# Four small tables padded in SBUF, so that every large tile begins on a multiple of 512 bytes

## The chip, the core and the metric

The kernel runs on one core of a Trainium2 chip. The metric is the time of one execution on the device, in microseconds. TensorE (PE; its weight loads are PEld) multiplies, VectorE (DVE), ScalarE (ACT) and GpSimd (POOL) do the element-wise work, and SyncE (SP), ACT and POOL issue DMA transfers, which 16 DMA engines carry out. SBUF is the on-chip memory, 128 partitions wide; an address below is a byte offset within each partition.

## The reference

Two layers follow each other. The first is a retention layer over 4 sequences of 768 steps, with 8 heads of width 64, and a state that decays by a factor gamma of its own for each head:

```python
for t in range(S):
    state = gamma[None, :, None, None] * state + np.einsum('bhd,bhe->bhde', k[:, :, t], v[:, :, t])
    y[:, :, t] = scale * np.einsum('bhd,bhde->bhe', q[:, :, t], state)
```

Its output, as 3072 rows of 512, goes through a feed-forward layer with a hidden width of 2048, whose negative hidden values are scaled by a factor `alpha` for each hidden column:

```python
h = x @ w_in
g = np.maximum(h, 0.0) + alpha * np.minimum(h, 0.0)
return g @ w_out
```

## The kernel before, in words

**Tiling.** The 3072 rows are twelve units of 256 steps, three to a sequence, and six blocks of two units. A unit is not walked step by step. Keys and queries are scaled by powers of gamma out of a table `tab` (`rescale`, line 145, tile `kdq`, f16), turned so that the head width lies on the partitions (tile `kq`), and multiplied with each other (`score_mm`, line 250). A mask in the table `mi` keeps the causal half (`masks`, line 263). The output of the unit is the masked scores times the values plus the queries times the state so far (`out_mm`, lines 281 and 296); the state is updated once for each half unit from key-value products (`sum_mm`, line 208; `state`, lines 228 to 238, tiles `ss`, `tf`, `tg`). `mi` also holds the identity for TensorE's transposes.

**Feed-forward.** Each block goes through `ffn1` (line 324; in halves, `ffn1_unit`, line 364, for block 1) with `w_in` as the stationary operand, an activation on ACT and one DVE instruction that uses `oma_sb` (one minus alpha), and then `ffn2` (line 395) with `w_out`, an ACT copy (line 404, tile `os`) and a store of 256 KB (line 408).

**Turning.** Units 0 to 3 are turned on TensorE (`turn_pe`, line 175, with an ACT copy, line 181). Units 4 to 11 are turned by a DMA transpose of the whole `kdq` tile into `kq` (`turn_dma`, line 165), which SP issues.

**Order.** The order is written out by hand (`manual_schedule`): the instructions of each engine run in the order of the code, and generators (`gen`, `half`, advanced by `tick`) put the feed-forward matmuls of one block between the retention work of the next. SP's queue holds, in this order, the loads of k, q and v for the units (line 125), the DMA transposes and the stores. POOL's queue holds rescales, state copies and the issue of the weight loads, which turn f32 into f16 on the way (lines 421 and 425). ACT's queue begins with the loads of `tab`, `mi` and `alpha` (lines 429 to 431). Around the second place that the prediction speaks of, the order on SP is: transpose of unit 4, loads of unit 6, the last three stores of block 0, transpose of unit 5, loads of unit 7.

**Placement.** All SBUF tiles come from one pool, which lays them one behind the other in the order of their creation, each rounded up to 32 bytes; the first lies at 16512. In the program before, the tiles begin here:

| tile | bytes per partition | begins at | past a multiple of 512 |
|---|---|---|---|
| tab | 208 | 16512 | 128 |
| mi | 768 | 16736 | 352 |
| alpha | 512 | 17504 | 96 |
| spin | 1024 | 18016 | 96 |
| warm | 4 | 19040 | 96 |
| oma | 64 | 19072 | 128 |
| win | 16384 | 19136 | 192 |

`wout`, the tiles `tg`, and all the buffers for loads, `kdq`, `kq`, `vx`, `xT`, `gt`, `hm`, `os` and the others follow `win`. Each of them is a multiple of 512 bytes, so each begins 192 bytes past a multiple of 512.

**What a DMA moves.** A load of k, q or v moves runs of 512 bytes (two steps of one head, f32) into a partition's row of 4096. A store moves rows of 2048 bytes out of `os`. A DMA transpose moves pieces of 256 bytes. A weight load reads runs of 1024 or 2048 bytes and writes half of that.

Of the kernel before, what the change touches and what calls it, by code (L numbers as in the profile page):

```python
# [9 lines left out]
FP = mybir.dt.float32  # L10
F16 = mybir.dt.float16
# [7 lines left out]
def kernel(  # L19
# [13 lines left out]
    NFT = d_ff // 128  # L33
# [10 lines left out]
    p_ar = np.arange(128, dtype=np.float64)  # L44


    OQ, OD, OI = 2 * H, 4 * H, 4 * H + NP
    NTAB = OI + NFT
    tab_np = np.zeros((128, NTAB), dtype=np.float64)
    for h in range(H):  # L50
        for r in range(2):
# [6 lines left out]
    tab_np[0:NFT, OI : OI + NFT] = np.eye(NFT)  # L58
    tab_np = tab_np.astype(np.float32)

    mi_np = np.zeros((128, 384), dtype=np.float16)
    pm = (p_ar % 64)[:, None]
    for rj in range(2):
        for ri in range(2):
# [7 lines left out]
    sbp = ctx.enter_context(tc.tile_pool(name="sbp", bufs=1, space=bass.MemoryType.SB))  # L72
    psp = ctx.enter_context(tc.tile_pool(name="psp", bufs=1, space=bass.MemoryType.PSUM))
    ctx.enter_context(tc.manual_schedule())

    tab = sbp.tile([128, NTAB], FP, tag="tab", name="tab")
    mi = sbp.tile([128, 384], F16, tag="mi", name="mi")
    mask = mi[:, 0:256].rearrange("p (r i) -> p r i", r=2)
    ident = mi[:, 256:384]
    dec = tab[:, OD : OD + NP].unsqueeze(2).to_broadcast([128, NP, 64])  # L80
    alpha_sb = sbp.tile([NFT, 128], FP, tag="alpha", name="alpha")
    spin = sbp.tile([128, 512], F16, tag="spin", name="spin")
    warm = sbp.tile([128, 1], FP, tag="warm", name="warm")
    oma_sb = sbp.tile([128, NFT], FP, tag="oma", name="oma")
    w_in_all = sbp.tile([128, 4, d_ff], F16, tag="win", name="win")
    w_out_all = sbp.tile([128, NFT, d_model], F16, tag="wout", name="wout")

# [539 lines left out]
```

## Time and profile before

| | |
|---|---|
| time, median of 3 runs | 226.14 us (225.40, 226.14, 226.42) |
| the profiled execution | 225.29 us, of which the span from first to last instruction is 223.5 us |
| granted TensorE clock, mean | 0.981 |
| PE busy | 205.9 us (92%) |
| DVE, ACT, POOL busy | 117.5, 101.2, 81.5 us |
| DMA | 34.01 MB in 62791 packets, of which 18081 under 512 bytes |
| queue q1 (SP): loads, stores, transposes | 57696 packets, 29.37 MB, 52.1% of 16 engines' span |
| queue q0 (POOL): weights | 4752 packets, 4.19 MB, 12.5% |
| queue q10 (ACT): tab, mi, alpha | 320 packets, 0.13 MB, 0.3% |

The span is drawn in 40 slices of 5.6 us; a digit is a busy share in tenths. PEclk is the share of its full clock that TensorE was granted. A packet is one contiguous piece of a transfer on one DMA engine; the DMA share of a stretch can exceed 1, since packets on one engine overlap. The chain is the work that ended last, followed back from the end of the program: at each step to what released it. An idle time in brackets is that of the engine just before the instruction, with what ended it.

### The profile page before, as it was taken

The page shows a single profiled execution, that of the slowest core. Times are in us where ns is not written, and L with a number is a line of the kernel's source. Part 1 is how long each engine was busy: PE and PEld are TensorE (multiplying, and loading weights), DVE is VectorE, ACT ScalarE, POOL GpSimd, SP SyncE. Part 2 cuts the span into 40 slices and gives each one's busy share as a digit, 9 for nine tenths or more (in the row PEclk, how much of TensorE's full clock was granted, in tenths as well). Part 3 has the DMA queues.
Part 4 walks back from the last instruction along what each step waited for, and adds up shares of the span by engine and source line. Part 5 has one row for each costly group of instructions (what it writes and reads, how often), then busy time and mean ns, then how long its engine had stood idle before and what let it go on. Part 6 is the DMA issues. An engine that isn't in the chain of part 4 may idle for free.

```text
span 223.5 us, 5019 instructions
## 1 busy us (share of the span) xinstructions
PE 205.9 (92%) x2100; PEld 109.7 (49%) x2100; DVE 117.5 (53%) x194; ACT 101.2 (45%) x168; POOL 81.5 (36%) x104
## 2 busy tenths in 40 slices
PE   7766798979899995999999999999999999999992
PEld 2445543547657743444455544545544555444440
DVE  3573198555753862118884058764088832388000
ACT  2544576425737513157613366414466242676121
POOL 2499302262039787800039920069700340000000
PEclk9998899999999999799999999999999999999998
DMA  6999999945696999939992169981190021100111
GB/s 183 298 182 123 204 226 276 245 83 94 163 290 165 198 325 215 269 92 237 242 261 96 49 142 269 219 221 47 62 218 5 4 91 53 47 3 0 47 73 68
DMA packets 62791, 34.01 MB, mean 152 GB/s; under 512 B 18081, under 2 KB 59697, under 8 KB 62769
## 3 DMA queue, kind: packets, MB, share of 16 engines
q1 hardware_dynamic: 57696, 29.37, 52.1%
q0 software_dynamic: 4752, 4.19, 12.5%
q8 instruction: 16, 0.26, 0.5%
q10 hardware_dynamic: 320, 0.13, 0.3%
q14 instruction: 7, 0.05, 0.1%
HBM read 27.40 MB, written 6.29 MB: 151 GB/s over the span
## 4 chain that ended last, share of the span: by engine, by line
PE 80%; DMA 6%; ACT 5%; POOL 4%; SPq 2%; issue 1%; DVE 1%; DVEq 0%; ACTq 0%; POOLq 0%
PE ops L395 34%; PE hps L324 31%; PE hps L364 6%; DMA kq<-kdq 3%; PE y L296 3%; DMA qs<-in_q_dram 2%; PE y L281 2%; SPq L125 2%; PE st L208 2%; ACT xT L309 2%; ACT kq L181 1%; PE sca L250 1%; ACT vx L159 1%; POOL kdq L145 1%; POOL tg L238 1%
## 5 line engine op out<-in xcount | busy, mean ns | idle before, releaser
L395 PE MATMUL ops<-wout,gt 128*128 128x512 f16 x384 | 89.5, 385 | 0.6 <-DVE gt L335 0.6
L335 DVE SCALAR_TENSOR_TENSOR gt<-hm,oma,hps 128x512 f16<-128x512 f32 x80 | 59.3, 747 | 43.4 <-ACT hm L334 35.5
L324 PE MATMUL hps<-xT,win 128*128 128x512 f16 (+1 forms) x336 | 71.1, 373 | 1.4 <-ACT xT L309 1.4
L395 PEld LDWEIGHTS <-gt 128*128 128x128 f16 x384 | 36.4, 99 | 43.2 <-issue 3.2
L334 ACT ACTIVATE hm<-hps 128x512 f32<-128x512 f32 x80 | 47.5, 597 | 20.7 <-PE hps L324 20.6
L324 PEld LDWEIGHTS <-win 128*128 128x128 f16 x336 | 33.3, 99 | 37.9 <-issue 1.4
L404 ACT ACTIVATE os<-ops 128x512 f32<-128x512 f32 x24 | 14.2, 599 | 59.7 <-PE ops L395 59.7
L145 POOL TENSOR_TENSOR kdq<-qs,tab 128x512 f16<-128x512 f32 (+1 forms) x16 | 24.4, 1528 | 19.8 <-DMA qs<-in_q_dram 19.7
L238 POOL CAST tg<-tf 64x256 f16<-64x256 f32 x40 | 16.2, 405 | 35.7 <-DVE tf L228 33.8
L263 DVE TENSOR_TENSOR m<-sca,mi 128x512 f16<-128x512 f32 x24 | 16.5, 686 | 23.1 <-PE scb L250 23.1
L232 POOL TENSOR_TENSOR tf<-ss,tab 128x256 f32<-128x256 f32 x16 | 9.8, 610 | 42.3 <-DVE ss L231 41.5
L309 ACT ACTIVATE xT<-y 128x512 f16<-128x512 f32 x24 | 16.0, 738 | 18.7 <-PE y L296 18.7
L376 DVE SCALAR_TENSOR_TENSOR gt<-hm,oma,hps 128x256 f16<-128x256 f32 x32 | 14.0, 478 | 8.3 <-ACT hm L374 8.2
L263 DVE TENSOR_TENSOR m<-scb,mi 128x512 f16<-128x512 f32 x24 | 16.3, 681 | 0.0
L145 POOL TENSOR_TENSOR kdq<-ks,tab 128x1024 f16<-128x1024 f32 x8 | 15.2, 1902 | 1.9 <-DMA ks<-in_k_dram 1.6
L364 PE MATMUL hps<-xT,win 128*128 128x256 f16 x128 | 14.3, 273 | 0.4 <-ACT xT L309 0.4
L181 ACT ACTIVATE kq<-trb 128x512 f16<-128x512 f16 x16 | 8.8, 595 | 12.2 <-PE trb L175 12.2
L364 PEld LDWEIGHTS <-win 128*128 128x128 f16 x128 | 12.5, 98 | 2.5 <-issue 0.7
L250 PE MATMUL sca<-kq 64*64 64x128 f16 x192 | 8.3, 218 | 4.5 <-DMA kq<-kdq 2.3
L374 ACT ACTIVATE hm<-hps 128x512 f32<-128x512 f32 x16 | 9.6, 597 | 5.4 <-PE hps L364 5.4
L231 DVE TENSOR_TENSOR ss<-tf,st 128x256 f32<-128x256 f32 x16 | 6.6, 415 | 8.3 <-PE st L208 5.7
L250 PEld LDWEIGHTS <-kq 64*64 64x64 f16 x384 | 6.6, 106 | 7.2 <-ACT kq L181 3.1
(30 smaller groups left out, 95.1 us busy)
## 6 DMA issues: line engine op xcount, KB each, us to landing
out_dram<-os SPq DMA_DIRECT2D x24, 256.0 KB, 2.3
vs<-in_v_dram SPq DMA_DIRECT2D x10, 512.0 KB, 6.9
ks<-in_k_dram SPq DMA_DIRECT2D x8, 512.0 KB, 4.6
qs<-in_q_dram SPq DMA_DIRECT2D x8, 512.0 KB, 5.8
ks<-in_k_dram SPq DMA_DIRECT2D x8, 256.0 KB, 5.5
qs<-in_q_dram SPq DMA_DIRECT2D x8, 256.0 KB, 5.2
wout<-in_moe_w_out_dram POOLq DMA_DIRECT2D x4, 512.0 KB, 10.7
win<-in_moe_w_in_dram POOLq DMA_DIRECT2D x3, 512.0 KB, 8.8
```

The lines of the kernel that those rows point to most:

```text
L145: eng.tensor_tensor(out=kdq[:, t, :, h0:h1, :].rearrange("p r h d -> p h r d"), in0=staged[u]["kq"[t]][:, h0:h1, :].rearrange("p h (r d) - ...
L238: nc.gpsimd.tensor_copy(out=o, in_=i)
L250: nc.tensor.matmul(out=scs[a][rows(c), at : at + 128], lhsT=kv[rows(a), 0, r, p, rows(c)], rhs=qmove(kq, a, c, p), start=True, stop=True,)
L263: nc.vector.tensor_tensor(out=m2, in0=live[u, hh][a].rearrange("p (r a i) -> p r a i", r=2, a=2), in1=mask.unsqueeze(2).to_broadcast([128, ...
L309: nc.scalar.activation(out=xT[n][:, :, at : at + 128].rearrange("k a (p r) -> k a r p", r=2), in_=ys[c].rearrange("k (a r p) -> k a r p", ...
L324: nc.tensor.matmul(out=hpss[ft][:, lo:hi], lhsT=w_in_all[:, hp, 128 * ft : 128 * ft + 128], rhs=xT[n][:, hp, lo:hi], start=(hp == 0), stop ...
L334: nc.scalar.activation(out=hm, in_=hps, func=RELU, bias=0.0, scale=-1.0)
L335: nc.vector.scalar_tensor_tensor(out=gt[:, ft, :], in0=hm, scalar=oma_sb[:, ft : ft + 1], in1=hps, op0=MULT, op1=ADD,)
L364: nc.tensor.matmul(out=hps[:, U * f : U * f + U], lhsT=w_in_all[:, hp, 128 * (f0 + f) : 128 * (f0 + f) + 128], rhs=xT[n][:, hp, cols], sta ...
L376: nc.vector.scalar_tensor_tensor(out=gt[:, f0 + f, cols], in0=hm[:, U * f : U * f + U], scalar=oma_sb[:, f0 + f : f0 + f + 1], in1=hps[:, ...
L395: nc.tensor.matmul(out=opss[tq], lhsT=gt[:, ft, 128 * tq : 128 * tq + 128], rhs=w_out_all[:, ft, :], start=(ft == 0), stop=(ft == NFT - 1),)
L404: nc.scalar.activation(out=os_sb, in_=opss[tq], func=COPY, bias=0.0, scale=1.0)
```

## The change

`tab` gets 96 columns instead of 52, `mi` 512 instead of 384, and `warm` and `oma` are made as tiles of 128 f32 columns of which the kernel uses 1 and 16. What is added is zeros or is not used. Every access keeps its shape, except that the loads of `tab` and `mi` carry the wider rows: 384 bytes a partition instead of 208, and 1024 instead of 768. The tiles then begin at 16512 (tab), 16896 (mi), 17920 (alpha), 18432 (spin), 19456 (warm), 19968 (oma) and 20480 (win); the last is 40 x 512, and `win` and all tiles behind it move up by 1344 bytes. No instruction is added, taken out or moved in any queue.

```diff
     OQ, OD, OI = 2 * H, 4 * H, 4 * H + NP
-    NTAB = OI + NFT
+    NTAB = 96
...
-    mi_np = np.zeros((128, 384), dtype=np.float16)
+    mi_np = np.zeros((128, 512), dtype=np.float16)
...
-    mi = sbp.tile([128, 384], F16, tag="mi", name="mi")
+    mi = sbp.tile([128, 512], F16, tag="mi", name="mi")
...
-    warm = sbp.tile([128, 1], FP, tag="warm", name="warm")
-    oma_sb = sbp.tile([128, NFT], FP, tag="oma", name="oma")
+    warm = sbp.tile([128, 128], FP, tag="warm", name="warm")[:, 0:1]
+    oma_sb = sbp.tile([128, 128], FP, tag="oma", name="oma")[:, 0:NFT]
```

## The prediction

> **What bounds the kernel now.** I read the page's slices first, then the chain that ended last, then windows of busy time and DMA rate, then the queue of SP.
>
> ```profile
> PE   7766798979899995999999999999999999999992
> PEclk9998899999999999799999999999999999999998
> DMA  6999999945696999939992169981190021100111
> ...
> PE 80%; DMA 6%; ACT 5%; POOL 4%; SPq 2%; issue 1%; DVE 1%; DVEq 0%; ACTq 0%; POOLq 0%
> ```
>
> A slice is 5.6 us. From slice 17 on (95 us) TensorE is full; before it there are two dips, in slices 1 to 5 and in slice 16, and the DMA row is full beside both. The pieces of the chain say what the two stretches are worth:
>
> ```profile
> 5.45 5.38 DMA qs<-in_q_dram
> ...
> 80.06 7.23 DMA kq<-kdq
> ...
> 160.37 13.81 PE hps L324 x64
> ```
>
> The last piece is 64 matmuls of 512 columns in 13.81 us, 215.8 ns each: from 95 us to the end TensorE is at its rate, and nothing that moves tiles about can be worth anything there. (Columns of the window rows below: stretch, its length, busy time of PE, PEld, DVE, ACT and POOL, granted clock, DMA share, GB/s.)
>
> ```profile
> 61.00:67.00 6.00, 5.99 (x125) 3.33 (x117) 3.23 (x6) 1.94 (x4) 1.63 (x4) 1.00 1.22 290
> 77.00:78.00 1.00, 1.00 (x61) 0.60 (x61) 0.55 (x2) 0.00 (x0) 0.11 (x1) 1.00 1.11 330
> 82.00:83.00 1.00, 1.00 (x6) 0.43 (x5) 0.00 (x0) 0.00 (x0) 0.89 (x3) 1.00 1.01 378
> 85.00:86.00 1.00, 0.06 (x6) 0.00 (x0) 0.00 (x0) 0.90 (x2) 1.00 (x2) 1.00 0.98 218
> 24.00:30.00 6.00, 4.58 (x48) 2.93 (x37) 3.05 (x5) 4.59 (x8) 0.43 (x2) 1.00 1.24 205
> 13.60:17.00 3.40, 2.14 (x72) 1.53 (x75) 2.24 (x4) 1.20 (x2) 3.25 (x6) 1.00 1.14 129
> 17.00:20.40 3.40, 1.54 (x59) 1.20 (x48) 1.71 (x3) 2.32 (x4) 3.29 (x6) 1.00 0.95 127
> 85.30:88.70 3.40, 1.37 (x36) 0.88 (x37) 0.91 (x2) 1.13 (x2) 2.92 (x3) 1.00 0.99 252
> ```
>
> The first five rows are five kinds of transfer, each alone: loads of k, q and v (pieces of 512 bytes) at 290 GB/s, the same loads in the first microsecond of a burst at 330, stores of results (2048 bytes) at 378, the DMA transpose (256 bytes) at 218, and the weights, read as 2048 bytes of f32 and written as 1024 of f16, at 205 written and so 410 read. Over 16 engines a piece takes 28.2, 24.8, 86.7, 18.8 and 79.9 ns. The last three rows explain the clock: TensorE stood idle for 1.26 us of the first, 1.86 of the second and 2.03 of the third, and after the second and third the clock is halved for 3.4 us (20.4 to 23.8 and 88.7 to 92.1), after the first it is not.
>
> ```profile
> 71.45 2.90 SPq L165 DMA_TRANSPOSE kq<-kdq  x1
> 74.46 0.53 SPq L125 DMA_DIRECT2D ks<-in_k_dram  x1
> 75.05 0.57 SPq L125 DMA_DIRECT2D qs<-in_q_dram  x1
> 75.67 1.69 SPq L125 DMA_DIRECT2D vs<-in_v_dram  x1
> 77.45 2.50 SPq L408 DMA_DIRECT2D out_dram<-os  x3
> 80.06 5.20 SPq L165 DMA_TRANSPOSE kq<-kdq  x1
> ...
> 87.91 6.61 PE L395 MATMUL ops<-wout,gt 128*128 128x512 f16 x22
> ```
>
> SP's queue runs without a break from 71.45, when unit 4's operands are ready, to the second transpose (unit 5's). An issue that should take 0.5 us takes 1.7, and the second transpose 5.2 where the shortest of the eight takes 1.89: the queue waits for bytes. That transpose lands at 87.29; unit 5's scores need it, TensorE is done with everything else at 85.06, and so idles 2.27 us; the half clock that follows makes 22 matmuls take 6.54 us on the chain where 22 x 215.8 ns is 4.75.
>
> **The change, part by part.** No instruction is added, removed or moved. Two tables carry more bytes, and every large tile goes from 192 bytes past a multiple of 512 to 0 past it.
>
> *Bytes.* tab grows from 208 to 384 bytes a partition, mi from 768 to 1024: 128 x 432, 55 KB more, on ACT's queue ahead of the first loads. At the 294 GB/s of the window from 5 to 13 us that is 0.19 us for what shares the engines. tab must be there for the first rescale at 3.94 us, which waits for k in any case; mi for TensorE's first transpose at 7.11, and it takes 3.0 us from its issue at 1.14. So +0.19 us at most, through the loads alone; I take all of it. The lower end is 0. Memsets and the warm-up keep their sizes; a view of 1 or 16 columns costs what the tile did.
>
> *Engine operands.* Before, all starts are multiples of 64 bytes, and distances between the large tiles stay as they are. The steady matmul at 215.8 ns is the row for TensorE, and 512 columns at a clock of 1.00 leave it nothing to gain. For DVE, ACT and POOL I take 0; past 95 us they have slack (DVE busy 53%, ACT 45%, POOL 36% of the span), and before it a 1% change on the 10% of the span, 22 us, that the chain spends on them would be 0.2 us either way.
>
> *DMA.* This is where it can matter. A piece of 512 bytes that starts 192 past a boundary of 256 touches three blocks of 256, an aligned one two; 256 bytes touch two and then one; 2048 touch nine and then eight. Against the rows: 28.2, 18.8 and 86.7 ns are 9.4, 9.4 and 9.6 ns per block touched. A cost of 9.4 ns per block fits all three. But so does 9.4 ns per 256 bytes and a fixed 9.4 per piece, since all these tiles share one offset. Two rows lean against the fixed cost: the weights take 79.9 ns for 2048 bytes read from a source that starts on its boundaries, hardly over 8 x 9.4 = 75.2 (their written side, five blocks, is hidden beneath), and in the first microsecond of a burst a 512-byte piece passes in 24.8. One leans for it: tab's 208-byte pieces follow each other at 13 ns in the packet records though each touches two blocks. So I bound an aligned 512-byte piece between 18.8 ns (two blocks) and 28.2 (nothing gained), and take 24.8, the nearest row that the same transfer reaches; a transpose's piece between 9.4 and 18.8, and take 14.1, the middle, since no row is nearer to either end; a store's between 78 and 86.7, and take 80.
>
> [...]
>
> *The start.* Of the loads before the 10.83 us landing, those from 6 us on run at the slow rate: 4.8 us x (1 - 24.8/28.2) = 0.6 us earlier, and 1.6 at the 18.8 end. With the tables' 0.19 the net is -0.4 us (ends +0.19 and -1.4). It reaches the end because POOL, which waits at 10.90 for that landing, then works without a gap to 16 us and releases the products with the state.
>
> *The second dip.* Between 71.45 and 87.29 the engines move two transposes, three loads of 512 KB and three stores. Saved: loads 5.4 us at the slow rate x 0.12 = 0.65; stores 2.0 x 0.08 = 0.15; the two transposes move at the steady 18.8 ns for 1.8 us each (their first microsecond is a start-up that I leave), x 0.25 = 0.9. Sum 1.7 of the 2.27 us; ends 0 and all 2.27 (more is cut off, since TensorE is late next, with its own work to 85.06). With 0.55 us idle instead of 2.03 the window behind it is far under the 1.26 after which the clock stayed, so the 1.8 us of slow matmuls go too.
>
> *Elsewhere nothing.* The other six transposes land 9 us or more before their scores; loads of later units are three units ahead; the weights are read-bound at 410 GB/s and their read side does not move. The store that ends the kernel takes 2.3 us; 8% of its moving part is under 0.1.
>
> Sum: -0.4 - 1.7 - 1.8 = -3.9 us. The profiled execution is 225.29 us (span 223.5 and 1.8 around it), 0.85 under the median of the three shown, so I take the sum off the median: 226.14 - 3.9 = 222.2 us. At the 18.8 and 9.4 ns ends: -1.4 - 2.27 - 1.8 = -5.5, or 220.7.
>
> **The rivals.** *The pieces cost the same wherever they start* (fixed cost per piece): 226.14 + 0.2 = 226.3 us, or within the 225.3 to 226.4 that the runs show. For it: tab's 13 ns, and that one offset can't show a dependence on offsets. Against it: the weights' 79.9 ns.
>
> *Only the loads gain, not the transposes*: -0.4, -0.8 and then an idle of 1.5 us, between the 1.26 that kept the clock and the 1.86 that lost it; 224.9 with the half clock, 223.1 without. It lies inside the forecast's range.
>
> [...]
>
> **How the numbers follow.** Under 0.5% (1.1 us) a measurement of this kernel can't tell from no change. Forecast, DMA pieces cheaper when aligned: 0.58 (0.10 of it with the loads alone), 220.7 to 224.9. Pieces cost the same: 0.27, 225.1 to 227.0. Slower by the clock or some price of the new places that no row shows: 0.15, about 228. So faster 0.58, same 0.27, slower 0.15. The range from 220.7 to 227.0 leaves out the slower case and little else; the forecast's own is 220.7 to 224.9.
>
> **What would show it.** Right: loads over 300 GB/s where they now hold 290, the transposes over 218, the second dip's idle under 1 us, no half clock near 90 us, and the 10.83 landing earlier. The steady matmul stays at 215.8 ns. Wrong: 290 and 218 unchanged, and with them the idle of 2.3 us; or faster transfers but the clock halved again, since its stretches may fall otherwise on what idle remains.

## The result and the profile after

The changed kernel takes 223.31 us (median of 17 executions, 221.92 to 225.62) beside 226.00 us for the kernel before in the same comparison (225.26 to 227.42): a ratio of 0.9871, with a 95% interval from 0.9839 to 0.9902. It is faster by 1.3%. Two of its 17 executions (225.41 and 225.62 us) count as slow and are left out of the ratio, so that it isn't simply 223.31 over 226.00 (0.988). The profiled execution took 222.22 us, with a span of 220.4.

First the page of the changed kernel: clock and the queue of SP. (Line numbers are higher by one after the change.)

```profile
PEclk9995999999999999999999999999999999999999
...
q1 hardware_dynamic: 57696, 29.37, 47.0%
```

The same 57696 packets of SP's queue hold the engines for 47.0% of a shorter span, where it was 52.1%. There is no half clock around 90 us any more; the one at the start is still there, and longer (6.8 us, from 15.7 to 22.5 us). Now the windows, in the columns of before: loads alone, transpose alone (two rows), stores alone.

```profile
63.00:66.00 3.00, 2.99 (x72) 1.65 (x74) 1.95 (x4) 0.60 (x1) 0.91 (x3) 1.00 1.16 351
84.00:84.90 0.90, 0.85 (x37) 0.58 (x34) 0.00 (x0) 0.48 (x2) 0.90 (x1) 1.00 1.28 289
97.50:98.50 1.00, 1.00 (x7) 0.43 (x5) 0.89 (x2) 0.78 (x2) 0.00 (x0) 1.00 1.27 290
91.00:92.00 1.00, 1.00 (x23) 0.70 (x24) 0.00 (x0) 0.00 (x0) 1.00 (x1) 1.00 1.04 398
```

Loads went from 290 GB/s to about 347 (351 in this window holds some 1% of other traffic), so a 512-byte piece takes 23.6 ns of an engine instead of 28.2. Stores went from 378 to 398 in the windows read, but that shows no gain from the new places: the window of 378 held a few other packets, and in e5 (below), where `os` stays at 192, stores alone ran as fast:

```profile
82.00:83.00 1.00, 1.00 (x6) 0.41 (x5) 0.09 (x1) 0.00 (x0) 0.85 (x3) 1.00 1.06 402
```

Of the transposes more below. The second dip in SP's and TensorE's timeline:

```profile
79.11 4.80 SPq L166 DMA_TRANSPOSE kq<-kdq  x1
...
85.96 0.24 PE L251 MATMUL sca<-kq 64*64 64x128 f16 x1 [1.11 <-DMA kq<-kdq]
86.53 4.92 PE L396 MATMUL ops<-wout,gt 128*128 128x512 f16 x22
```

and the chain, where the three pieces that the prediction used stand again:

```profile
5.18 5.46 DMA qs<-in_q_dram
...
25.46 11.42 PE hps L325 x60
...
79.11 6.80 DMA kq<-kdq
...
86.60 4.85 PE ops L396 x22
...
188.81 13.81 PE hps L325 x64
```

Three lines of the kernel before that belong beside these:

```profile
25.68 11.42 PE hps L324 x60
...
87.97 6.54 PE ops L395 x22
```

```profile
87.33 0.24 PE L250 MATMUL sca<-kq 64*64 64x128 f16 x1 [2.27 <-DMA kq<-kdq]
```

The two chains, laid side by side, give the whole difference of the spans. The long run of the first feed-forward matmuls begins at 25.46 us instead of 25.68: 0.2 us from the start. Unit 5's scores begin at 85.96 instead of 87.33: 1.2 us more, which is the idle time going from 2.27 to 1.11 us. (In the two other profiles with all large tiles aligned and nothing added, e1 and e3, it is 1.53 and 1.47 us, so this one is the shortest of three.) The 22 matmuls behind take 4.85 us instead of 6.54: 1.7 us from the clock. Together 3.1, and 223.5 - 220.4 is 3.1. From there on nothing differs: 64 matmuls take 13.81 us in both.

### The profile page after: what moved, and what is told of

It reads as the page before. It is cut to its first block, busy times and chain, and to the rows that moved or that the text cites. A ratio compares the mean times of both kernels' runs of the same rounds, so it can differ in the third digit from the quotient of the medians.

```text
span 220.4 us, 5019 instructions
## 1 busy us (share of the span) xinstructions
PE 204.5 (93%) x2100; PEld 109.7 (50%) x2100; DVE 117.4 (53%) x194; ACT 101.2 (46%) x168; POOL 81.1 (37%) x104
## 3 DMA queue, kind: packets, MB, share of 16 engines
q1 hardware_dynamic: 57696, 29.37, 47.0%
## 4 chain that ended last, share of the span: by engine, by line
PE 81%; DMA 6%; ACT 5%; POOL 3%; SPq 2%; issue 1%; DVE 1%; DVEq 0%; ACTq 0%; POOLq 0%
PE ops L396 33%; PE hps L325 32%; PE hps L365 6%; PE y L297 3%; DMA kq<-kdq 3%; DMA qs<-in_q_dram 2%; PE y L282 2%; SPq L126 2%; PE st L209 2%; ACT xT L310 2%; ACT kq L182 1%; PE sca L251 1%; ACT vx L160 1%; POOL kdq L146 1%; POOL tg L239 1%
## 5 line engine op out<-in xcount | busy, mean ns | idle before, releaser
L396 PE MATMUL ops<-wout,gt 128*128 128x512 f16 x384 | 87.8, 379 | 0.6 <-DVE gt L336 0.6
L396 PEld LDWEIGHTS <-gt 128*128 128x128 f16 x384 | 35.9, 98 | 42.0 <-issue 0.9
```

What stands on the lines that cost most here:

```text
L396: nc.tensor.matmul(out=opss[tq], lhsT=gt[:, ft, 128 * tq : 128 * tq + 128], rhs=w_out_all[:, ft, :], start=(ft == 0), stop=(ft == NFT - 1),)
```

## The experiments

My theory: what counts is where the tiles that a DMA writes or reads begin, by a boundary of 256 bytes; the clock is a second gain on top, decided by the idle time that the DMA leaves. The rivals: the wider tables themselves, a boundary of 512, a price that grows with the distance from the boundary, and a gain that is the clock's alone.

### Tables or tiles

**e1_spacer**: the tables of before and a spare tile.

```diff
+    sbp.tile([128, 160], F16, tag="gap", name="gap")   # 320 bytes
     w_in_all = sbp.tile([128, 4, d_ff], F16, tag="win", name="win")
```

> The four tables keep their sizes of before; a spare tile of 320 bytes ahead of the input weights alone brings them and all tiles behind to a multiple of 512. Theory (what counts is where the large tiles begin): the gain of the change, about 223 us against 226, loads at 346 GB/s and transposes at 289 as in the changed kernel, and since the 55 KB of wider tables are gone up to 0.2 us less. Rival (the wider tables do it, by their own rows or by what they delay): about 226 us, loads at 290 GB/s.

**e2_off192**: the changed kernel with a spare tile of 192 bytes at the same place.

```diff
+    sbp.tile([128, 96], F16, tag="gap", name="gap")   # 192 bytes
     w_in_all = sbp.tile([128, 4, d_ff], F16, tag="win", name="win")
```

> The changed kernel with a spare tile of 192 bytes behind the padded tables: wide tables, but all large tiles at 192 past a multiple of 512 again. Theory (place of the tiles): back to the kernel before, 226 to 226.4 us, loads at 290 GB/s, transposes at 218. Rival (the wider tables): about 223 us.

Measured: e1 took 222.79 us, ratio 0.9891 (0.9848 to 0.9934); e2 took 226.66 us, 1.0006 (0.9964 to 1.0048). The windows of loads alone are, for e1 and then for e2:

```profile
63.00:66.00 3.00, 2.99 (x72) 1.64 (x74) 1.95 (x4) 0.60 (x1) 0.91 (x3) 1.00 1.16 350
```

```profile
63.00:66.00 3.00, 3.00 (x60) 1.44 (x58) 1.59 (x4) 0.78 (x3) 0.79 (x2) 1.00 1.22 290
```

The spare tile alone brings the whole gain, as far as the intervals can tell, and the wide tables without the places bring none of it. The tables' size is settled as no cause.

### Which boundary

**e3_off256**, **e4_off64**, **e9_off32**, **e10_off128**: the edit of e2 with a spare tile of 256, 64, 32 and 128 bytes.

> The changed kernel with all large tiles at 256 past a multiple of 512. Theory (a piece pays for one block of 256 bytes more when it begins off a boundary of 256): as the changed kernel, about 223 us, 346 and 289 GB/s. Rival (a multiple of 512 is needed): loads of 512 bytes at 290 GB/s again and about 226 us.

> The changed kernel with all large tiles at 64 past a multiple of 512. Theory (one block more costs the same wherever the boundary falls in the piece): as the kernel before, 290 and 218 GB/s, about 226 us. Rival (the first block is paid for from its beginning, so the price grows with the distance from the boundary, 64 bytes costing a third of 192): loads near 325 GB/s, transposes near 260, about 224 us. Second rival (only a multiple of 64 matters, which the kernel before already had, and something else in the layout helped): about 223 us.

> The changed kernel with all large tiles at 32 past a multiple of 512. Theory (one block of 256 more costs the same wherever the boundary falls): loads at 290 GB/s, transposes at 214 to 218, as at 64 and 192. Rival (off a multiple of 64 a write costs more): both rates clearly lower still.

> The changed kernel with all large tiles at 128 past a multiple of 512. Theory (the same price at every place off a boundary of 256): loads at 290 GB/s, transposes at 214 to 218. Rival (128 is a boundary of its own): 346 and 289.

Measured: e3 took 222.59 us, ratio 0.9858 (0.9786 to 0.9929); e4 226.64 us, 1.0018 (0.9981 to 1.0055). e9 and e10 ran once each, 226.76 and 223.98 us, and are read for their rates, not their times. Loads alone at 256, 64, 32 and 128 past a multiple of 512, in this order:

```profile
63.00:66.00 3.00, 3.00 (x66) 1.70 (x64) 1.59 (x4) 1.08 (x2) 0.34 (x1) 1.00 1.15 347
```

```profile
63.00:66.00 3.00, 3.00 (x66) 1.76 (x65) 1.59 (x4) 1.08 (x2) 0.18 (x1) 1.00 1.17 290
```

```profile
63.00:66.00 3.00, 3.00 (x66) 1.72 (x65) 1.59 (x4) 1.09 (x2) 0.22 (x1) 1.00 1.16 290
```

```profile
63.00:66.00 3.00, 3.00 (x61) 1.46 (x58) 1.59 (x4) 0.78 (x3) 0.78 (x2) 1.00 1.20 291
```

256 is as good as 512, and 32, 64, 128 and 192 are equally bad. For the transposes too: unit 6's ran at 215, 214 and 215 GB/s at 32, 64 and 128 (e9, e4, e10), at 214 at 192 (before) and at 290 at 256 (e3). The price of being off a boundary of 256 is a step here, not a slope: 4.6 ns for a 512-byte piece (28.2 ns where an aligned one takes 23.6) at each of the four places. That a start further past the boundary costs more does not show in these runs (loads at 290 GB/s at 32 and at 192). A load only writes a moved tile, while a transpose reads one and writes another; both show the step, from 347 to 290 GB/s and from 290 to 214.

### Which transfers

**e5_loads** and **e6_turns**: the kernel before, with only one group of buffers moved, by a spare tile of 320 bytes ahead of the group and one of 192 behind it, so that all others stay at 192.

```diff
+    sbp.tile([128, 160], F16, tag="gap", name="gap")
     load(0, ("k0", "q0", "k1", "q1", "v0", "v1"))
+    sbp.tile([128, 96], F16, tag="gap2", name="gap2")
```

```diff
+    sbp.tile([128, 160], F16, tag="gap", name="gap")
+    unit(0)
+    sbp.tile([128, 96], F16, tag="gap2", name="gap2")
     rescale(V, 0, 0, 0, 4)
```

> The kernel before, with the load buffers of k, q and v alone moved to a multiple of 512 by spare tiles; weights, kdq, kq, os and the rest stay at 192. Theory (each kind of transfer gains by its own buffer): loads at 346 GB/s, transposes still at 218 and stores at 378; of the 15.9 us between unit 4's operands and unit 5's scores the loads' 0.65 us are gained and the transposes' are not, so an idle of 1.5 to 1.7 us, 224.5 to 225.5 us. Rival (the loads carry nearly all of the gain, since they are 18.9 of the 29.4 MB): about 223 us.

> The kernel before, with kdq, kq and vx alone moved to a multiple of 512; the load buffers and the rest stay at 192. Theory (each kind gains by its own buffer): transposes at 289 GB/s, loads at 290; an idle of 1.3 to 1.5 us before unit 5's scores, 224.5 to 225.5 us. Rival (the transposes hold all of the gain, since it is a transpose that unit 5's scores wait for): about 223 us.

Measured: e5 224.04 us, ratio 0.9915 (0.9887 to 0.9943); e6 224.79 us, 0.9938 (0.9896 to 0.9980). Idle before unit 5's scores: 1.96 us in e5, 1.86 in e6. For each, the window of loads alone and one of the transpose of unit 6 alone, e5 first:

```profile
63.00:66.00 3.00, 3.00 (x60) 1.37 (x58) 1.60 (x4) 0.78 (x3) 0.79 (x2) 1.00 1.15 347
99.90:100.90 1.00, 1.00 (x6) 0.49 (x5) 0.93 (x2) 0.73 (x2) 0.00 (x0) 1.00 1.13 206
```

```profile
63.00:66.00 3.00, 3.00 (x67) 1.72 (x65) 1.59 (x4) 1.09 (x2) 0.03 (x1) 1.00 1.22 291
100.20:101.20 1.00, 1.00 (x7) 0.46 (x5) 0.89 (x2) 0.78 (x2) 0.00 (x0) 1.00 1.27 289
```

Each kind of transfer follows its own buffers: the loads are fast in e5 and slow in e6, the transpose the other way round. The times fall between before and after in both, and neither holds the whole gain; both waits came out longer than expected (1.5 to 1.7 and 1.3 to 1.5 us), and e5's time lower. How they share it I can't settle from these two: the idle time before unit 5's scores runs from 2.04 to 2.82 us in the five profiles with nothing aligned and nothing added (before, e2, e4, e9, e10), and 1.96 and 1.86 lie just under that.

But e5 and e6 sent me back to the transpose's own row, and there a step of the prediction falls. These are two windows of the kernel **before**, the first 0.3 us later than the one that the prediction read as 218 GB/s:

```profile
85.30:86.30 1.00, 0.00 (x0) 0.00 (x0) 0.00 (x0) 1.00 (x2) 1.00 (x2) 1.00 1.27 289
100.50:101.50 1.00, 1.00 (x6) 0.43 (x5) 0.89 (x2) 0.78 (x2) 0.00 (x0) 1.00 1.14 214
```

The transpose that unit 5 waits for moved at 289 GB/s without any alignment; the window from 85 to 86 had averaged it with the end of its start-up. By the packet records the middle half of the packets of the transposes of units 4 and 5 takes 0.92 us each in the kernel before, and 0.92 and 0.93 in the changed one. Others, such as unit 6's at 100 us, did run at 214 and now run at 290, and those nobody waits for.

Two things keep this from meaning that these two transposes had nothing to gain. From its first packet to its last, unit 4's took 2.97 us before and 2.48 after; the difference lies in its start-up, where it pauses (unit 5's took 3.40 and 3.55). And the high rate does not always come without alignment. In e8, the kernel before with added matmuls (next section), unit 4's transpose ran alone at the low rate; in e7, the changed kernel with the same matmuls, at the high one, and took 2.09 us instead of 2.68. First e8, then e7:

```profile
73.00:74.00 1.00, 1.00 (x12) 0.90 (x10) 1.00 (x3) 0.60 (x2) 1.00 (x2) 1.00 1.16 214
```

```profile
72.00:73.00 1.00, 1.00 (x12) 0.89 (x10) 1.00 (x4) 0.60 (x1) 1.00 (x1) 1.00 1.28 290
```

What e6 gained stays open: in its profile the two transposes took 3.04 and 3.30 us, hardly less than before, and the half clock fell otherwise (10.2 us at the start and none at 90 us, where the kernel before has 3.4 at each).

### The clock

**e7_keep_after** and **e8_keep_before**: matmuls on the constant tile `spin`, with a product that nobody reads, put where TensorE waits; in the changed kernel and in the one before. `keep(n, b)` runs n of them into PSUM bank b.

```diff
     turn_pe(1, 0, (2, 3))
+    keep(3, 4)
     score_mm(1, 0, (4, 5))
     masks(1, 0)
+    keep(2, 2)
     turn_pe(1, 1, (2, 3))
...
+    keep(6, 2)
     sum_mm(1, (2, 3))
...
     state(1, 1, G)
+    keep(5, 2)
     tick(gen)
...
+            if n == 1:
+                keep(4, 4)
             score_mm(u0 + 1, 0, (4, 5))
```

> The changed kernel with matmuls on a constant tile, whose product nobody reads, put where TensorE waits: 16 of them between 12 and 25 us and 4 ahead of unit 5's scores. Theory (what is left of the scatter between 222 and 225.6 us is the halved clock after the early waits): no stretch at half clock before the end, 220.5 to 221.5 us and a narrow spread. Rival (the scatter comes from the transfers): the spread stays, and the added matmuls cost up to 0.5 us.

> The kernel before with the same added matmuls. Theory (the change saves transfer time, and the clock is a second gain on top of it that the idle before unit 5's scores decides): no half clock here either, so 226 less 1.7 us at 90 us and less some 1.2 us at 20 us, 223 us; the changed kernel with the same matmuls stays 1.4 to 2 us below it, 1.2 of it in the wait before unit 5's scores. Rival (the gain of the change was the clock alone): both kernels with added matmuls take the same time within 0.3 us.

Measured: e7 221.62 us (221.16 to 222.01), ratio 0.9802 (0.9770 to 0.9833), 0.1 above the expected range; e8 223.01 us (222.81 to 223.10), ratio 0.9863 (0.9834 to 0.9891), as expected. The clock row, which is the same on both pages, and in e8's timeline the wait before unit 5's scores:

```profile
PEclk9999999999999999999999999999999999999999
...
84.69 1.04 PE L94 MATMUL kps<-spin 128*128 128x512 f16 x4
86.75 0.24 PE L250 MATMUL sca<-kq 64*64 64x128 f16 x1 [1.03 <-DMA kq<-kdq]
```

With the clock full in both, the scatter shrinks to 0.9 and 0.3 us, and what is left between them, 223.01 - 221.62 = 1.4 us, is what the faster transfers are worth by themselves, good to some 0.4 us: four executions each, and the kernel of e7, run again as e12, took 222.07. Executions without added matmuls agree: the kernel before (223.78) and e2 (223.80) each had one at a granted clock of 1.00, and the changed kernel's three at 0.996 and 0.997 took 222.08 to 222.64. The rival that the gain is the clock's alone would have had 0.3 at most. The rest of the change's 2.7 us, 1.3, I put down to the clock, which the shorter wait spares; it is a difference and not measured by itself. e7 also beats both kernels: 2.0% under the one before (1.5% as e12).

### The price of the wider tables

**e11_keep_spacer** (e1 with the matmuls of e7) and **e12_keep_wide** (e7 again), side by side.

> The narrow tables with the spare tile of 320 bytes, and the added matmuls that hold the clock. Theory (55 KB of wider tables cost the start up to 0.19 us): 0.1 to 0.2 us under the same with the wide tables, 221.4 us. Rival (the tables pass beside work that waits anyway): the same time as with the wide tables within 0.1 us.

> The changed kernel with the added matmuls once more, beside the one with narrow tables: 221.6 us, as it took before; the yardstick for the tables' bytes.

Measured: 221.80 us (221.28 to 221.93) and 222.07 us (221.56 to 222.37), both 0.4 to 0.5 above what was expected. The narrow tables lie 0.3 us lower, on the side that the theory has, but the two ranges overlap by more than that, so the price of the 55 KB stays unresolved.

## Why the prediction came out right, step by step

*The mechanism* was right in the main: pieces of loads and transposes that begin off a boundary cost more, the second dip shrinks, and the half clock behind it goes. The main number was 1.1 us low (222.2 against 223.31). Of the signs that it named, one did not come: the dip's idle is 1.11 us and not under 1. And "the transposes over 218" tells little of the path, since the two on it were over 218 before, in their steady part.

*The price of a piece.* 24.8 ns was taken for an aligned 512-byte piece; 23.6 was measured. For a store 80 was taken against 86.7, and no gain is shown (402 GB/s, or 81.5 ns, off the boundary in e5). The reading behind it, 9.4 ns for each block touched, does not fit: of the 9.4 ns in question a load's piece lost 4.6 and a transpose's 4.7 (18.8 to 14.1), and the rest stayed. The two accounts that the prediction set against each other, a price for the extra block and a fixed price, were each about half true. For the transpose 14.1 was the middle of two bounds, and that it came so close is luck. The weights, which were to gain nothing, gained nothing: 203 GB/s written from 23 to 27 us before, 191 after. That it is their read side that bounds them is the prediction's reading, and no run parts the two sides.

*The step that failed: the second dip, in its transposes.* "... the two transposes move at the steady 18.8 ns for 1.8 us each (their first microsecond is a start-up that I leave), x 0.25 = 0.9." In the profile they moved at 14.1 ns already once started, as the 85.3 to 86.3 window above shows. By the packet records the dip, from the first packet of unit 4's transpose to the last of unit 5's, took 14.07 us before and 12.92 after, 1.15 less. Unit 4's transpose gave 0.49 of it, in the start-up that the prediction left out; from there to the last packet of unit 6's loads 0.73 was saved, where 0.65 stood; and behind them, where the stores were to give 0.15 and unit 5's transpose 0.45, nothing (4.75 and 4.80 us). So the dip gained 1.2 us, where the sum was 1.7. How much of the 0.49 is alignment isn't settled: unit 4's transpose took 2.66 to 3.04 us in the other profiles where it was aligned (e1, e3, e6) and 2.83 to 3.34 where it was not (e2, e4, e5, e9, e10). With added matmuls it was 2.03 to 2.09 (e7, e11, e12) against 2.68 (e8).

*The start.* -0.4 us was forecast and -0.2 measured. The 8th load landed at 10.64 us instead of 10.83. The engines do move faster there too (325 GB/s from 5 us to the landing, 297 before), but only from some 6 us on, and the tables' 0.19 us comes off that; how much of it they really take is argued, not shown (e11 and e12).

*The clock.* The 22 matmuls gave 1.7 us in the profile, 1.8 forecast. But that is one execution. What the clock is worth over many is some 1.3 us, as what e7 and e8 leave of the 2.7, since a half-clock stretch at the start may be 3.4, 6.8 or 10.2 us long (before, e5 and e10: 3.4; after, e1 and e2: 6.8; e3, e4, e6 and e9: 10.2), and the changed kernel's own executions still scatter over 3.7 us for it. The term was mis-sized by treating a thing that falls differently from execution to execution as certain; with the dip's 0.5 us and the start's 0.2 that is the 1.2 us between the sum of 3.9 and the measured 2.7.

*The rivals.* "The pieces cost the same wherever they start" falls with e2 and e3. "Only the loads gain" is wrong as it stands, since aligned transposes run at 290 GB/s where they ran at 214; but on the path they gained less than forecast, and its 223.1 without the half clock is nearer to what came than the main number is. The result lies in both ranges and doesn't part the two. The slower case did not come: the slowest of the changed kernel's 17 executions took 225.62 us, and no run shows the 228 that stood for it. The stretch at half clock at the start is longer in the profile of the changed kernel, 6.8 us for 3.4, but e2, e4 and e9, with nothing aligned, have 6.8 and 10.2 too, so it isn't shown that the change makes it longer.

## What to carry to other kernels

Where DMA is on the path, look at where the tiles begin and not only at their sizes: one odd small table at the front puts every large buffer behind it off a boundary of 256 bytes, and 512-byte pieces then move at 290 instead of 347 GB/s here; one spare tile repairs it without touching a table (222.79 us in e1). A rate read from a single microsecond may average a start-up with a steady flow, so slide the window before costing a step by it. And where a wait of TensorE is followed by a halved clock, price the two apart: matmuls into a bank that nobody reads took the clock out of the comparison here, and on the kernel before were worth as much as the change (a ratio of 0.9863 in e8, 0.9871 for the change).

## What the runs showed that I had not expected

- Off the boundary there are two rates for the same transfer. Loads of the kernel before moved at 330, 314 and 290 GB/s in the microseconds from 77, 78 and 79 us, and at 347, 306 and 288 in those from 87.8, 88.8 and 89.8; its transposes at 289 (from 85.3) or 214 (from 100.5). On the boundary the loads hold 347 and the transposes 290 where they run alone. Why the lower one sets in after a while is not shown by any run here.
- The length of one wait does not decide the halved clock. Before unit 5's scores an idle of 1.86, 1.96 and 2.04 us (e6, e5, e10) left the clock full and 2.24, 2.27, 2.45 and 2.82 us (e4, before, e9, e2) was followed by a halved one; but in the changed kernel it was halved at 15.65 us, and no wait in the 3.41 us ahead of that was longer than 0.72. The clock changed in steps of 3.41 us: in the kernel before it was halved from 20.41 to 23.82 and from 88.68 to 92.09 us, with 64.85 us, 19 such steps, between the two, and in the changed kernel from 15.65 to 22.48, two steps. Counted off in these steps from the first halved one, backwards and forwards up to the last matmul, the idle time sorts the steps in the profiles of the two kernels: the steps at full clock ahead of a halved one have 1.86 and 2.06 us in the kernel before and 2.10 in the changed one, and of those that full clock followed, none has more than 1.42 and 1.41. (At half clock 1.46 us, from 15.65 in the changed kernel, was followed by half clock again.) The nearest pair stands in e10, in the two rows below: 3.41 - 1.64 is 1.77 us, and the clock was halved next; 3.41 - 1.66 is 1.75, and it stayed. In e10 the wait of 2.04 us was parted between two steps, 0.29 and 1.75 us. Where the steps fall differs between executions: one begins at 85.27 us in the kernel before and at 83.92 in the changed one. What sets the clock is not shown by any run here.

```profile
17.69:21.10 3.41, 1.64 (x46) 1.34 (x42) 1.71 (x3) 2.08 (x4) 3.30 (x7) 1.00 1.03 155
85.96:89.37 3.41, 1.66 (x37) 0.99 (x38) 1.20 (x2) 1.07 (x2) 2.86 (x3) 1.00 1.00 255
```
